# One chunk's transpose moved from TensorE to the DMA crossbar, and the last output tile made in three column pieces

## The chip, the cores and the metric

The kernel runs on one core of a Trainium2 chip. The metric is device time in microseconds (us); lower is better. A core has a matrix engine (TensorE, PE in the profile; its weight loads are the row PEld), a vector engine (DVE), a scalar engine (ACT), GpSimd (POOL) and SyncE (SP). Each works through its own instruction list in order. SP and POOL also start DMA transfers; the transfers then run on the core's 16 DMA engines, beside everything else.

## The reference, cut to what matters

A decaying linear attention feeds a feed-forward block:

```python
# q, k, v: (4 batches, 8 heads, 768 positions, 64) float32
state = gamma[h] * state + k_t (outer) v_t           # per head
y_t   = q_t @ state / sqrt(64)
x     = y as (3072 tokens, 512)
h = x @ w_in                                         # 512 -> 2048
g = h + sin(alpha * h)**2 / (alpha + 1e-9)
out = g @ w_out                                      # 2048 -> 512, float32
```

## The kernel before, in words

The 3072 tokens are 24 chunks of 128, six per batch. Within a chunk the attention is a masked matrix product; between chunks a 64x64 state per head is carried. The list `order` (also called `P`) first names the first chunk of each batch and then the rest, so `P[4]` is the second chunk of batch 0. Chunks are taken in groups of 4, 2, 4, 4, 4, 4 and 2; the last group has the two token tiles that end the kernel.

For a chunk the steps are these:

- **load**: POOL starts one transfer each for q, k and v (L83), which also convert float32 to bf16. q and k of a chunk lie side by side in the tile `qkr`, which has one buffer for each chunk.
- **transpose** of q and k into `qkT` (six buffers in rotation). Two ways exist. `stage_T` (L190 to L200): eight 128x128 transposes on PE into a PSUM tile `pt` (L195), then one copy by DVE (L200) or ACT (L198). `turn` (L202 to L205): one DMA transpose, SBUF to SBUF, started by SP. Before the change the seventh and eighth chunk, `P[6]` and `P[7]`, still go by `stage_T`; from `P[8]` on all go by `turn`.
- **A** (`stage_A`): scores on PE (L213) from `qkT` into `pa`, masked by DVE into `aT` (L217).
- **M** (`stage_M`): the chunk's output on PE (L247, L251), then DVE writes it, scaled, into `xT` (L258), the transposed input of the feed-forward block. **S** adds to the state (L227), and ACT copies it (L234).

The feed-forward work of a group is a `phase`: it runs over slots of one or two 128-row blocks of the hidden layer. A slot has PE products into `ph` (L279), a sine (L282) and a square (L287) on ACT, and a fused multiply-add on DVE into `gT` (L294). Between slots stand the products of the group before with `w_out` (L304, `po`), 16 for each token tile. When a tile's sixteenth is done, `take` has ACT copy it to `o_sb` (L316; three buffers) and SP send it out (L317). The last tile of all is copied in two halves, one by DVE (L313) and one by ACT (L314), into one `o_sb`, and then leaves in one transfer.

The order of all engines' work is written out by hand. Around the change it is: the end of the first group's stage, with the product calls `F(...)` and the transposes of `P[4]` and `P[5]`; then the POOL loads of `P[7]` and on; then `phase(1, ...)`, whose table says which attention step stands in which slot: `T(P[6])` in slot 0, `A(P[6])` in slot 1, `T(P[7])` in slot 2, `A(P[7])` and `M(P[6])` in slot 3, `A(P[8])` and `M(P[7])` in slot 5. The entries `X(P[8])`, `X(P[9])` and so on are `turn` calls, two slots or more ahead of their A.

SP's list before is short: two loads and alpha at the start, the stores of the first three token tiles, then transposes and stores in turn.

Of the kernel before, what the change touches and what calls it, by code (L numbers as in the profile page):

```python
# [8 lines left out]
F32 = mybir.dt.float32  # L9
# [6 lines left out]
def kernel(  # L16
# [15 lines left out]
    nc = tc.nc  # L32
    B, H, S, D = q.shape
    C = 128
# [3 lines left out]
    d_model = H * D  # L38
    d_ff = moe_w_in.shape[1]
    KS = d_model // 128  # L40
    FF = d_ff // 128
# [7 lines left out]
    sizes = [4, 2, 4, 4, 4, 4, 2]  # L49
    assert sum(sizes) == NJ  # L50
    NG = len(sizes)
    groups = [order[sum(sizes[:g]):sum(sizes[:g + 1])] for g in range(NG)]
# [4 lines left out]
    work = ctx.enter_context(tc.tile_pool(name="work", bufs=2))  # L57
    psum = ctx.enter_context(tc.tile_pool(name="psum", bufs=1, space=bass.MemoryType.PSUM))
# [5 lines left out]
    w_out = big.tile([128, FF, d_model], BF16, name="w_out")  # L64
# [125 lines left out]
    def stage_T(j, eng=None, tag="ty"):  # L190
        pt = psum.tile([128, 2 * NP, 128], BF16, name="pt", tag=tag, bufs=4 if tag == "mm" else 1)
        st["qkT", j] = work.tile([128, 2 * NP, 128], BF16, name="qkT", tag="qkT", bufs=6)
        for i in range(2):
            for p in range(NP):
                nc.tensor.transpose(pt[:, i * NP + p, :],  # L195
                                    raw["qk"[i], j][:, 2 * p:2 * p + 2, :].rearrange("p h d -> p (h d)"), ident)
        if eng is nc.scalar:
            nc.scalar.copy(st["qkT", j], pt)  # L198
        else:
            nc.vector.tensor_copy(st["qkT", j], pt)  # L200

    def turn(j):  # L202

        st["qkT", j] = work.tile([128, 2 * NP, 128], BF16, name="qkT", tag="qkT", bufs=6)
        nc.sync.dma_start_transpose(out=st["qkT", j], in_=raw["qk", j].rearrange("p i h d -> p (i h d)"))  # L205

    def stage_A(j):
        qkT = st["qkT", j]
        pa = psum.tile([128, 2, NP, 128], F32, name="pa", tag="pa")
        for p in range(NP):  # L210
            for e in range(2):
                r = slice(64 * e, 64 * e + 64)
                nc.tensor.matmul(pa[:, e, p, :], qkT[r, NP + p, :], qkT[r, p, :],  # L213
                                 start=(p == 0), stop=True, skip_group_check=True)
        aT = work.tile([128, 2, NP, 128], BF16, name="aT", tag="aT", bufs=2)
        m = dec.rearrange("p e n t -> p (e n) t") if j % NCH == 0 else mask_bc
        nc.vector.tensor_mul(aT.rearrange("p e n t -> p (e n) t"), pa.rearrange("p e n t -> p (e n) t"), m)  # L217
        st["aT", j] = aT
# [17 lines left out]
    def stage_M(j):  # L236
        c = j % NCH
        g, i = place[j]
        if g not in xT:
            xT[g] = work.tile([128, KS, sizes[g] * C], BF16, name="xT", tag="xT", bufs=3)  # L240
        qkT, aT, vs = st["qkT", j], st["aT", j], raw["v", j]
        py = psum.tile([128, NP, 128], F32, name="py", tag="ty")
        if c > 0:
            for p in range(NP):
                for e in range(2):
                    r = slice(64 * e, 64 * e + 64)
                    nc.tensor.matmul(py[r, p, :], s_bd[c % 2][:, p, r], qkT[:, p, :],  # L247
                                     start=(p == 0), stop=True, skip_group_check=True)
        for p in range(NP):
            for e in range(2):  # L250
                nc.tensor.matmul(py[64 * e:64 * e + 64, p, :], vs[:, 2 * p + e, :], aT[:, e, p, :],  # L251
                                 start=(c == 0 and p == 0), stop=True, skip_group_check=True)
        x = xT[g][:, :, i * C:(i + 1) * C]
        if c == 0:
            nc.scalar.copy(x, py)
            return
        ps = stage_S(j) if c < NCH - 1 else None
        nc.vector.tensor_mul(x, py, qg[:, c])  # L258
        if ps is not None:
            keep_S(j, ps)  # L260


    gT = {}
# [33 lines left out]
    out_view = out.rearrange("(t p) n -> p t n", p=128)  # L297
# [3 lines left out]
    def ff_out(g, ts, f):  # L301
        if (g, ts) not in po:
            po[g, ts] = psum.tile([128, d_model], F32, name="po", tag="mm", bufs=4)
        nc.tensor.matmul(po[g, ts], gT[g][:, f, ts * C:(ts + 1) * C], w_out[:, f, :],  # L304
                         start=(f == 0), stop=(f == FF - 1))
        if f == FF - 1:
            take(g, ts)

    def take(g, ts):
# [6 lines left out]
            nc.scalar.copy(o_sb, po[g, ts])  # L316
        nc.sync.dma_start(out=out_view[:, groups[g][ts], :], in_=o_sb)  # L317

    def out_pieces(g, tss):
        return [lambda ts=ts, f=f: ff_out(g, ts, f) for ts in tss for f in range(FF)]  # L320

# [53 lines left out]
    def phase(g, outs, att, nf=1):  # L375

        no, done = len(outs), 0
        for n in range(FF // nf):
            now = Slot(g, n * nf, nf=nf).sq("A")
            for fn in att.get(n, ()):  # L380
                fn()
            now.add()
            while done < no * (n + 1) * nf // FF:
                outs[done]()
                done += 1

    def T(j):
        return lambda: stage_T(j)

    def X(j):  # L390
        return lambda: turn(j)

    def A(j):
        return lambda: stage_A(j)

    def M(j):
        return lambda: stage_M(j)

    def SK(j):
        return lambda: keep_S(j, stage_S(j))  # L400
# [3 lines left out]
    P = order  # L404
    n3, n4 = 3 * C, 4 * C
    def F(ts, fs):
        for f in fs:
            for t in ts:
                ff_out(0, t, f)

    def early(f, tag="mm"):
        return Slot(0, f, (0, n3), tag=tag)
# [10 lines left out]
    c = early(3)  # L423
# [10 lines left out]
    c = early(6)  # L434
# [45 lines left out]
    scale_v(P[4], nc.vector)  # L480
    F((0, 1), (13, 14))
    stage_T(P[5], nc.scalar, "mm")
    F((0, 1), (15,))


# [8 lines left out]
    for n in range(11, NJ + 2):  # L494
# [3 lines left out]
        if n in (13, 15):  # L498
            scale_v(P[(n - 9) // 2], nc.gpsimd)

    outs = out_pieces(0, (2, 3))

    def fill(n):
        for _ in range(n):
# [9 lines left out]
    stage_M(P[5])  # L514
    fill(4)
    phase(1, outs,
          {0: [T(P[6]), X(P[8])], 1: [A(P[6])], 2: [T(P[7]), X(P[9])], 3: [A(P[7]), M(P[6])], 4: [X(P[10])],
           5: [A(P[8]), M(P[7])], 6: [X(P[11]), A(P[9]), M(P[8]), SK(e1)], 7: [M(P[9])]}, 2)
    for g in range(2, NG):
        att = {}  # L520
        if g + 1 < NG:
            js = groups[g + 1]
            for i, j in enumerate(js):
                a = i * FF // len(js) + 1
                n = P.index(j) + 2
                if n < NJ:
                    att.setdefault(a + 1, []).append(X(P[n]))
                att.setdefault(a, []).append(A(j))
                if i > 0:
                    att[a].append(M(js[i - 1]))  # L530
                if j % NCH == 1:
                    att[a].append(SK(j - 1))
            att.setdefault(FF - 2, []).append(M(js[-1]))
        phase(g, out_pieces(g - 1, range(sizes[g - 1])), att, 1 if sizes[g] > 2 else 2)
    for fn in out_pieces(NG - 1, range(sizes[-1])):
        fn()
# [1 line left out]
_INS = ['q', 'k', 'v', 'moe_w_in', 'moe_w_out', 'moe_alpha']  # L538
_OUTS = [((3072, 512), 'float32')]
# [25 lines left out]
```

## Time and profile before

| what | value |
|---|---|
| median of 8 runs | 219.77 us (219.16 to 221.38) |
| the profiled execution: its own time | 218.79 us |
| its span, first to last instruction | 217.0 us |
| granted TensorE clock | 0.996 |
| PE busy | 204.5 us (94%) |
| ACT busy | 162.8 us (75%) |
| DVE busy | 128.2 us (59%) |
| POOL busy | 90.0 us (41%) |
| DMA moved | 24.67 MB |

The profile page has a row for each engine over the span cut in 40 slices, a chain of waits followed back from the last instruction, and rows for groups of instructions with their source line (L) and tile names. The time of the profiled execution is 1.79 us more than its span, which is what lies around the first and the last instruction. A timeline row reads: start, duration, engine, line, operation, output<-input, shape, count; and in brackets how long the engine was idle before, and which instruction released it. "SPq" is SP's queue of transfer-starting instructions; the length of such a row is the time that SP spends on starting, not the transfer itself. A transfer's time from issue to landing is given apart.

### The profile page before, as it was taken

The numbers are of one execution on the slowest core, as the hardware profiler recorded it, in microseconds if no ns is written. First come the engines' busy times: TensorE is split into PE (matmuls) and PEld (weight loads), VectorE is DVE, ScalarE is ACT, GpSimd is POOL, SyncE is SP. The second block draws the span as 40 slices with busy tenths as digits, with TensorE's granted clock in tenths as the row PEclk, the third lists the DMA queues.
The fourth block names the chain that finished last, engine by engine and source line by source line (L and its number), as shares of the span: only waits on it lengthen the run. The fifth ranks groups of instructions, "written<-read, shape, count | busy, mean of one in ns | idle before, by whom it ended". The sixth has DMA issues, their size and how long they took to land.

```text
span 217.0 us, 4218 instructions
## 1 busy us (share of the span) xinstructions
PE 204.5 (94%) x1634; PEld 108.0 (50%) x1661; DVE 128.2 (59%) x213; ACT 162.8 (75%) x311; POOL 90.0 (41%) x105
## 2 busy tenths in 40 slices
PE   7999898999989999999999999999999999999992
PEld 3545544467764545445454545454544544556540
DVE  4687669858895767766376466367464655233300
ACT  7679796658989899788768867777868876766610
POOL 8975336899699885994963000000000000000000
PEclk9999999999999999999999999999999999999998
DMA  9999999999999999999999047127011101111121
GB/s 129 152 192 190 205 207 166 154 206 180 154 145 188 162 130 163 110 150 169 133 173 134 17 97 100 47 51 98 15 37 51 48 0 51 48 48 48 51 96 49
DMA packets 99508, 24.67 MB, mean 114 GB/s; under 512 B 92304, under 2 KB 96416, under 8 KB 99488
## 3 DMA queue, kind: packets, MB, share of 16 engines
q0 software_dynamic: 77024, 13.37, 85.3%
q1 hardware_dynamic: 22464, 11.02, 26.7%
q8 instruction: 13, 0.21, 0.5%
q14 instruction: 7, 0.06, 0.1%
HBM read 27.27 MB, written 6.29 MB: 155 GB/s over the span
## 4 chain that ended last, share of the span: by engine, by line
PE 74%; DVE 10%; DMA 4%; POOL 4%; ACT 4%; issue 2%; POOLq 0%
PE po L304 35%; PE ph L279 31%; DVE gT L294 5%; DMA qkr<-in_k_dram 4%; PE py L247 3%; PE pa L213 2%; POOL qkr L83 2%; DVE aT L217 2%; PE py L251 2%; ACT s L282 1%; POOL vr L83 1%; DVE xT L258 1%; ACT s L287 1%; PE ps L227 1%; DVE s L289 1%
## 5 line engine op out<-in xcount | busy, mean ns | idle before, releaser
L294 DVE SCALAR_TENSOR_TENSOR gT<-s,rec_alpha,ph 128x512 bf16<-128x512 f32 (+3 forms) x120 | 74.2, 638 | 68.0 <-ACT s L287 67.4
L279 PE MATMUL ph<-xT,w_in 128*128 128x512 bf16 (+3 forms) x478 | 97.9, 336 | 1.1 <-DVE gT L294 0.7
L304 PE MATMUL po<-w_out,gT 128*128 128x512 bf16 x360 | 94.1, 379 | 3.8 <-issue 2.9
L282 ACT ACTIVATE s<-ph,alpha_sb 128x512 f32<-128x512 f32 (+3 forms) x120 | 69.6, 602 | 33.7 <-PE ph L279 33.5
L279 PEld LDWEIGHTS <-w_in 128*128 128x128 bf16 x480 | 45.6, 98 | 42.6 <-issue 2.4
L287 ACT ACTIVATE s<-s 128x512 f32<-128x512 f32 (+1 forms) x94 | 58.4, 621 | 2.6
L304 PEld LDWEIGHTS <-gT 128*128 128x128 bf16 x384 | 35.2, 98 | 38.2 <-issue 0.6
L112 POOL TENSOR_TENSOR vr<-vr,kg 128x512 bf16<-128x512 bf16 x21 | 22.0, 1058 | 13.4 <-DMA vr<-in_v_dram 13.4
L217 DVE TENSOR_TENSOR aT<-pa,mask 128x1024 bf16<-128x1024 f32 x20 | 24.4, 1222 | 0.3 <-PE pa L213 0.3
L83 POOL DMA_DIRECT2D vr<-in_v_dram x24 | 21.8, 910 | 3.1 <-DMA w_in<-in_moe_w_in_dram 1.7
L83 POOL DMA_DIRECT2D qkr<-in_q_dram x23 | 21.3, 927 | 3.9 <-DMA w_in<-in_moe_w_in_dram 1.7
L83 POOL DMA_DIRECT2D qkr<-in_k_dram x23 | 20.6, 894 | 3.8 <-DMA w_out<-in_moe_w_out_dram 3.4
L234 ACT CAST s_bd<-ps 64x256 bf16<-64x256 f32 x40 | 14.4, 360 | 2.5 <-PE ps L227 2.1
L316 ACT COPY o_sb<-po 128x512 f32<-128x512 f32 x23 | 13.1, 576 | 3.9 <-PE po L304 3.9
L258 DVE TENSOR_TENSOR xT<-py,qg 128x512 bf16<-128x512 f32 x20 | 13.7, 685 | 2.6 <-PE py L251 2.4
L328 PE MATMUL spare<-warm 128*128 128x512 bf16 x27 | 9.9, 490 | 1.4 <-DVE warm L131 1.2
L213 PEld LDWEIGHTS <-qkT 64*128 64x128 bf16 x192 | 5.4, 94 | 9.3 <-issue 7.1
L251 PE MATMUL py<-aT,vr 128*64 128x128 bf16 x192 | 9.5, 220 | 0.4 <-DVE rec_alpha L366 0.2
L213 PE MATMUL pa<-qkT 64*128 64x128 bf16 x192 | 9.5, 219 | 0.2
L247 PE MATMUL py<-qkT,s_bd 128*64 128x128 bf16 x160 | 8.3, 224 | 0.7 <-DVE xT L258 0.7
L247 PEld LDWEIGHTS <-s_bd 128*64 128x64 bf16 x160 | 5.4, 109 | 4.8 <-issue 2.0
L251 PEld LDWEIGHTS <-vr 128*64 128x64 bf16 x192 | 6.9, 110 | 1.3 <-issue 1.0
(59 smaller groups left out, 69.7 us busy)
## 6 DMA issues: line engine op xcount, KB each, us to landing
out_dram<-o_sb SPq DMA_DIRECT2D x24, 256.0 KB, 2.6
vr<-in_v_dram POOLq DMA_DIRECT2D x24, 128.0 KB, 6.7
qkr<-in_q_dram POOLq DMA_DIRECT2D x23, 128.0 KB, 5.8
qkr<-in_k_dram POOLq DMA_DIRECT2D x23, 128.0 KB, 6.2
w_in<-in_moe_w_in_dram POOLq DMA_DIRECT2D x4, 512.0 KB, 10.6
w_out<-in_moe_w_out_dram POOLq DMA_DIRECT2D x4, 512.0 KB, 14.6
q<-in_q_dram SPq DMA_DIRECT2D x1, 256.0 KB, 3.3
k<-in_k_dram SPq DMA_DIRECT2D x1, 256.0 KB, 4.3
```

The costliest lines, as they stand in the source:

```text
L83: nc.gpsimd.dma_start(out=t, in_=chunk_of(src, j))
L112: eng.tensor_mul(raw["v", j], raw["v", j], kg[:, j % NCH, :, None].to_broadcast([128, H, D]))
L213: nc.tensor.matmul(pa[:, e, p, :], qkT[r, NP + p, :], qkT[r, p, :], start=(p == 0), stop=True, skip_group_check=True)
L217: nc.vector.tensor_mul(aT.rearrange("p e n t -> p (e n) t"), pa.rearrange("p e n t -> p (e n) t"), m)
L247: nc.tensor.matmul(py[r, p, :], s_bd[c % 2][:, p, r], qkT[:, p, :], start=(p == 0), stop=True, skip_group_check=True)
L251: nc.tensor.matmul(py[64 * e:64 * e + 64, p, :], vs[:, 2 * p + e, :], aT[:, e, p, :], start=(c == 0 and p == 0), stop=True, skip_group_che ...
L258: nc.vector.tensor_mul(x, py, qg[:, c])
L279: nc.tensor.matmul(self.ph[:, m, :], w_in[:, i, f * 128:(f + 1) * 128], xT[g][:, i, self.lo:self.hi], start=(m == 0 and i == 0), stop=(i = ...
L282: nc.scalar.activation(out=self.s[:, m, :], in_=self.ph[:, m, :], func=ACTF.Sin, scale=alpha_sb[:, f:f + 1])
L287: nc.scalar.activation(out=self.s, in_=self.s, func=ACTF.Square)
L294: nc.vector.scalar_tensor_tensor(gT[self.g][:, f, self.lo:self.hi], self.s[:, m, :], rec_alpha[:, f:f + 1], self.ph[:, m, :], op0=ALU.mult ...
L304: nc.tensor.matmul(po[g, ts], gT[g][:, f, ts * C:(ts + 1) * C], w_out[:, f, :], start=(f == 0), stop=(f == FF - 1))
```

## The change

There are two edits. First, the transpose of `P[6]` leaves slot 0 of phase 1, where PE and DVE did it, and becomes a `turn` that stands in the program just before the last product call of the first stage. In SP's list it comes fourth: after alpha and ahead of all stores. It waits for the landing of q and k of `P[6]` and for its `qkT` buffer, which the first chunk used.

Second, the last token tile is no longer made as one tile of 512 columns but as three of 256, 128 and 128 columns, one after the other, each with its own 16 products over the hidden layer, its own copy (ACT for the first, DVE for the other two) and its own store.

```diff
+    def last_tile(g, ts):
+        lo = 0
+        for n in (d_model // 2, d_model // 4, d_model // 4):
+            c = slice(lo, lo + n)
+            lo += n
+            ph = psum.tile([128, n], F32, name="poh", tag="mm", bufs=4)
+            for f in range(FF):
+                nc.tensor.matmul(ph, gT[g][:, f, ts * C:(ts + 1) * C], w_out[:, f, c],
+                                 start=(f == 0), stop=(f == FF - 1))
+            o_sb = work.tile([128, d_model], F32, name="o_sb", tag="o_sb", bufs=3)[:, :n]
+            if n > d_model // 4:
+                nc.scalar.copy(o_sb, ph)
+            else:
+                nc.vector.tensor_copy(o_sb, ph)
+            nc.sync.dma_start(out=out_view[:, groups[g][ts], c], in_=o_sb)
...
     F((0, 1), (13, 14))
     stage_T(P[5], nc.scalar, "mm")
+    turn(P[6])
     F((0, 1), (15,))
...
-          {0: [T(P[6]), X(P[8])], 1: [A(P[6])], 2: [T(P[7]), X(P[9])], 3: [A(P[7]), M(P[6])], 4: [X(P[10])],
+          {0: [X(P[8])], 1: [A(P[6])], 2: [T(P[7]), X(P[9])], 3: [A(P[7]), M(P[6])], 4: [X(P[10])],
...
-    for fn in out_pieces(NG - 1, range(sizes[-1])):
+    for fn in out_pieces(NG - 1, range(sizes[-1] - 1)):
         fn()
+    last_tile(NG - 1, sizes[-1] - 1)
```

The `turn` that the first edit calls exists before:

```python
def turn(j):
    st["qkT", j] = work.tile([128, 2 * NP, 128], BF16, name="qkT", tag="qkT", bufs=6)
    nc.sync.dma_start_transpose(out=st["qkT", j], in_=raw["qk", j].rearrange("p i h d -> p (i h d)"))
```

## The prediction

> **What bounds the kernel now.** I read the engine rows first, then the chain of waits, then the two places that the change touches.
>
> ```profile
> PE 204.5 (94%) x1634; PEld 108.0 (50%) x1661; DVE 128.2 (59%) x213; ACT 162.8 (75%) x311; POOL 90.0 (41%) x105
> ...
> PE 74%; DVE 10%; DMA 4%; POOL 4%; ACT 4%; issue 2%; POOLq 0%
> ```
>
> PE is busy for 94% of the span and is 74% of the chain that ended last. Time is won by taking work off PE where the chain runs on it, or by shortening the tail behind its last product. The first place, in the chain in order of time:
>
> ```profile
> 46.87 0.97 PE po L304 x4
> 47.84 0.87 PE ph L279 x8
> 48.71 0.45 PE pt L195 x8
> 49.16 0.43 PE po L304 x2
> 49.59 0.87 PE ph L279 x8
> 50.47 0.33 PE pa L213 x8
> ```
>
> The row `pt` is the transpose of P[6]. It lies on the chain between PE pieces that follow without a gap, so its 0.45 us count in full. The row `pa` is A of P[6], the first reader of the transpose. The second place, in the timeline:
>
> ```profile
> 212.28 0.59 PE L304 MATMUL po<-w_out,gT 128*128 128x512 bf16 x2
> 212.91 0.42 DVE L313 COPY o_sb<-po 128x256 f32<-128x256 f32 x1 [6.23 <-PE po L304]
> 213.37 0.37 ACT L314 COPY o_sb<-po 128x256 f32<-128x256 f32 x1 [3.33 <-DVE o_sb L313]
> 213.77 0.33 SPq L317 DMA_DIRECT2D out_dram<-o_sb  x1
> ```
>
> PE ends at 212.87. The two half copies run one after the other, not side by side: ACT starts 0.04 us after DVE ends. So 0.90 us pass between the last product and the store's issue. The span ends 3.2 us later.
>
> **Part 1: the transpose.** Removed on PE: eight products, 0.45 us on the chain. Removed on DVE: one copy of 128x1024 (0.69 us at 49.20); in this stretch DVE waits for ACT (0.40 us at 50.28), so that alone is worth nothing. ACT waits 0.24 to 0.29 us for PE in each of these slots, and so follows PE forward. A of P[6] would be due on PE at 50.39 - 0.45 = 49.94, if its input is there.
>
> Added: one DMA transpose on SP. It waits for q and k of P[6]; POOL issued k at 35.31 and it took 7.0 us to land, so 42.31 (q: 32.76 + 8.7 = 41.46). The buffer it waits for is old. The nearest case, P[9], had k at 45.33 + 5.9 = 51.23 and its transpose started at 51.31, 0.08 later; so here the start is 42.39. Behind it on SP stand the first two stores (issued at 42.99 before). SP spends 1.24 to 2.6 us on starting a transpose, so they slip by 0.6 to 2.0 us. Nobody feels it: PSUM is freed by ACT's copy, and a fourth use of the three `o_sb` buffers comes only at 64.99. The third store (48.49) and the transpose of P[8] behind it (49.00) keep their place.
>
> When does it land? The query of the transpose nearest in time (49.0, of P[8]) says:
>
> ```profile
> L205 SPq DMA_TRANSPOSE qkT<-qkr x1: 1613/1613/1613, 49.0 to 49.0; - x1
> ...
> DMA to landing us min/median/max: 7.9/7.9/7.9
> ```
>
> The others between 51 and 81 us took 5.7 to 7.5; those after 115, with the DMA engines nearly idle, 3.1 to 5.2. At 42.39 the engines are as full as at 49 (loads moved at a steady 154 GB/s from 36 to 46 us; a load takes 6.2 to 7.4 us to land). **Here a rule speaks otherwise**: the Trainium skill (Advanced Engine Details and Errata, X-Bar Transpose) says that transposing DMAs on this chip are as fast as ordinary ones. An ordinary one of the same 256 KB, the store at 42.99, took 5.5; by the rule the transpose lands at 47.9 and A never waits (gain 0.45). The rows say that a transpose is slower: 3.1 to 5.2 against the 2.0 of a store in quiet, 7.9 against 4.1 of the store issued 0.5 us before it at 48.49. I take the row: 42.39 + 7.9 = 50.3. The lower end is 5.7 (48.1). The upper end is the slowest quiet one plus what the crowd added to the store: 5.2 + (5.9 - 2.0) = 9.1 (51.5).
>
> So A of P[6] waits 50.3 - 49.94 = 0.36 us on PE, in order, with the `po` and `ph` of slots 1 and 2 queued behind it; of the 0.45 won, 0.09 stay. Ends: 0.45 won, or 51.5 - 50.39 = 1.1 lost.
>
> The second cost is on the next transposes. The new one moves 256 KB more; of one in quiet I see about 1.3 us of moving at 205 GB/s. The engines are shared until 57, where P[8]'s transpose lands (49.00 + 7.9 = 56.9) while its A starts on PE at 57.62, and at 57.5 with 0.09 us won. If the whole 1.3 us reach it, it lands at 58.2 and PE waits 0.7; if half, at 57.55, and it waits 0.05. DVE needs these scores only at 58.75, 0.72 us after PE had them, since it is busy itself, and that takes up much. I take 0.1, ends 0 and 0.7. P[9] (51.31 + 7.3 = 58.6, due at 60.06) has 1.4 us, P[10] (56.95 + 6.3 = 63.2) is due at 66.8. The loads of P[7] (k at 38.12 + 6.9 = 45.0, used at 52) bear it.
>
> Part 1 in sum: 0.45 - 0.36 - 0.1 = nothing; ends 0.45 won and 1.8 lost. What is won or lost here shifts all that follows, since no transfer bounds the chain after it.
>
> **Part 2: the tail.** On PE 16 products of 512 columns at 216 ns (18 `po` in 4.06 us) are 3.46 us. In their place come 16 of 256 at 108 ns (`ph` of slots with two blocks: eight in 0.87) and 32 of 128. For these the first stage has a row with the same weights and width:
>
> ```profile
> 24.88 1.06 PE L279 MATMUL ph<-xT,w_in 128*128 128x128 bf16 x16
> ```
>
> (1.06 - 0.22)/15 = 56 ns, 0.22 being one product alone. **A rule speaks against the change here**: the Trainium skill (TensorE: Matmul & The Clock Gate, Back-to-back issue gap) gives 81 ns for a sustained stream of weight load and 128-column product, and 56 only for one without the weight load. This row has a weight load for each product and still shows 56, in a run of 16; the new run is 32 long. By the row: 1.73 + 1.79 = 3.52, 0.06 more than before. By the rule: 1.73 + 2.59 = 4.32, 0.86 more, which would eat the gain. I take the row.
>
> The last product then ends at 212.93. DVE's copy of 128x128 isn't in the trace; from 0.42 (128x256) and 0.69 (128x512, `xT`) it is some 0.29. With 0.03 and 0.04 us between engines the last store is issued at 213.29, not 213.77: 0.48 won. The first two pieces' copies and stores lie under later products (their stores at about 211.6 and 212.4, 0.33 each on SP). The third piece's `o_sb` is the one that tile 0's store read, issued at 210.1 and landed 2.0 later, at 212.1, before the copy at 212.96.
>
> The last transfer shrinks from 256 KB, which the trace shows moving for 0.70 us, to 64 KB, in 128 rows of 512 B where it had 2 KB. At the same rate that is 0.18; no row shows 512 B rows here, and if they cost half again to twice as much, 0.27 to 0.36. I take 0.30, so 0.40 won; the ends are 0 (time goes by rows, not bytes) and 0.52. What follows the data (0.4 us to landing, about 1.2 us of ending) stays. Part 2: 0.48 + 0.40 = 0.9 won; ends 0.45 and 1.0 by the rows, 0.1 by the rule.
>
> **Sum.** 218.79 - 0.0 - 0.9 = 217.9 for an execution like the profiled one. That one lies 0.98 under the median of 219.77, so the median goes to about 218.9; I say 219.0, a gain of 0.8 us (0.35%). A measurement of this kernel can tell about 0.5%, 1.1 us, from no change.
>
> **The rivals.**
> 1. *The transpose is in time* (landing by 49.9, 7.5 us after issue). For it: most rows of the busy time are 5.7 to 7.5. Against: none of those stood in front of so many loads. 0.45 + 0.9 = 1.35 won: 218.4.
> 2. *The transpose becomes the wait* (slower than before). Place: the first weight load of A of P[6] on PE, behind which slots 1 and 2 stand. Price: each us of landing past 49.94 is one us of PE. It decides when it takes away the tail's 0.9 too, past 51.3 (8.9 us after issue); slower by 1.1 from 52.4. For it: loads ahead of it in the engines, and the stores issued beside it moved no data until about 46. Against: nothing in the trace took over 7.9. At the upper ends (1.8 lost, 0.9 won) the median is 220.7.
> 3. *The tail gives nothing*: 32 short products at 81 ns. Then 0.1 won with part 1 at nothing: 219.7. Against it is the row of 16.
> 4. *The last store is no shorter* than before: part 2 is 0.5, median 219.3, still no change that can be told.
>
> **Numbers.** Forecast 0.40, rival 1 0.23, rival 2 0.22, rival 3 0.07, rival 4 0.08. Faster by over 0.5%: most of rival 1 and a little of the forecast's edge, 0.26. Slower: the far part of rival 2, 0.19. The rest 0.55. The range goes from rival 1 with the best tail (219.77 - 0.45 - 1.0 = 218.3, less 0.3 for the spread of medians, 218.0) to rival 2 at its upper ends, 220.8.
>
> **What would show it.** In the profile after: no `pt` at 48.7 on PE; SP's transpose at about 42.4 with a landing near 7.9; a wait of PE on L213 near 50 us of 0.3 to 0.4 (0 in rival 1, over 1.5 in rival 2); A of P[8] waiting 0 to 0.2; the last 32 products in about 1.8 us (2.6 in rival 3); the last store issued 0.36 us after PE's end, and the span ending about 2.8 us after that. The forecast is wrong if A of P[6] waits over 1 us, or if the time from PE's end to the span's end does not shrink from 4.1 to about 3.2.

## The result, and the profile after

The changed kernel takes 218.35 us (median of 20 runs, 217.5 to 219.33) where the kernel before takes 219.58 (55 runs). The ratio is 0.9941, with a 95% interval of 0.9926 to 0.9957: 0.6% faster, 1.2 to 1.3 us. 219.0 was forecast, a gain of 0.8. The 0.5% that was named as the least that can be told from no change lies inside the interval's gains of 0.43 to 0.74% (the medians alone give 0.9944).

Where it came from can be read to a tenth of a microsecond, once the profiled execution is cut at three events that both kernels have. They are the first `ph` product of phase 1, the first `ph` product of the next group, and ACT's copy of the last tile but one. "Start" is all before the first event; the tail ends with the span, which is printed to a tenth, so tails are good to 0.05 us.

| profiled execution | start | stage (phase 1) | middle | tail | span |
|---|---|---|---|---|---|
| before | 47.68 | 16.87 | 144.91 | 7.54 | 217.0 |
| changed | 48.62 | 16.72 | 144.90 | 6.46 | 216.7 |

The spans alone mislead. The changed kernel's profiled execution had a start that was 0.94 us longer and still ended 0.3 us sooner. The start varies from execution to execution with or without the edits: three other kernels below that have the first edit started at 47.68 to 47.70, and two that do not have it there, e1 and e5, at 48.26 and 48.80. Without it the gains are 0.15 in the stage and 1.08 in the tail, 1.23 in sum, as in the medians (219.58 - 218.35 = 1.23; that they agree to the hundredth is chance).

**The stage.** PE's weight loads from `qkT` in the changed kernel's timeline, for A of P[6], P[7], P[8] and P[9]. The bracket is the idle time of the weight loads and what ended it:

```profile
50.89 0.23 PEld L213 LDWEIGHTS <-qkT 64*128 64x128 bf16 x8 [0.21 <-issue]
...
54.67 0.22 PEld L213 LDWEIGHTS <-qkT 64*128 64x128 bf16 x8 [0.50 <-DVE qkT L200]
...
58.57 0.22 PEld L213 LDWEIGHTS <-qkT 64*128 64x128 bf16 x8 [0.37 <-DMA qkT<-qkr]
...
61.29 0.23 PEld L213 LDWEIGHTS <-qkT 64*128 64x128 bf16 x8 [0.50 <-DMA qkT<-qkr]
```

and before the change, for P[6] and P[7]:

```profile
50.39 0.23 PEld L213 LDWEIGHTS <-qkT 64*128 64x128 bf16 x8 [0.21 <-issue]
...
53.89 0.23 PEld L213 LDWEIGHTS <-qkT 64*128 64x128 bf16 x8 [0.21 <-DVE qkT L200]
```

An idle time of 0.21 us stands before A even where nothing was waited for ("issue"): A then starts 0.97 us after the first of the `ph` products just ahead of it, without a gap on PE. So only what lies above 0.21 is delay.

A of P[6] did not wait for its transpose. It ran 2.27 us after the stage began, where it was 2.71 before (50.39 - 47.68): the whole 0.44 were won there. The transpose itself was quick:

```profile
L205 SPq DMA_TRANSPOSE qkT<-qkr x1: 1347/1347/1347, 43.8 to 43.8; - x1
...
DMA to landing us min/median/max: 6.6/6.6/6.6
```

43.84 + 6.6 = 50.4, some 0.45 us before A of P[6] started. But A of P[7] then stood at 0.50, for the DVE copy of the other PE transpose. That is a delay of 0.29 us, and 0.15 us of the gain were left (54.67 - 48.62 = 6.05 against 53.89 - 47.68 = 6.21). DVE's own timeline says why the copy could not come sooner. In the changed kernel:

```profile
51.23 0.87 DVE L294 SCALAR_TENSOR_TENSOR gT<-s,rec_alpha,ph 128x256 bf16<-128x256 f32 x2 [2.81 <-ACT s L287]
52.02 1.22 DVE L217 TENSOR_TENSOR aT<-pa,mask 128x1024 bf16<-128x1024 f32 x1
53.15 0.86 DVE L294 SCALAR_TENSOR_TENSOR gT<-s,rec_alpha,ph 128x256 bf16<-128x256 f32 x2
53.93 0.69 DVE L200 COPY qkT<-pt 128x1024 bf16<-128x1024 bf16 x1
```

and before, the first and the last of these four:

```profile
50.28 0.87 DVE L294 SCALAR_TENSOR_TENSOR gT<-s,rec_alpha,ph 128x256 bf16<-128x256 f32 x2 [0.40 <-ACT s L287]
...
52.99 0.68 DVE L200 COPY qkT<-pt 128x1024 bf16<-128x1024 bf16 x1
```

DVE first sat for 2.81 us, because its next instruction waits for the first slot's sine and square. These depend on a `ph` product that stands ahead of the removed transpose, so nothing made them earlier. From there DVE worked without a gap through these rows to the copy. Counted from the stage's begin, the first of them starts at 2.61 us (2.60 before) and the copy ends at 6.00 (5.99 before). PE had come forward; DVE had not. Before, A of P[7] started at 6.21, so this copy had about 0.2 us to spare; the 0.44 us that PE won were more than that, and the rest became the delay.

**The tail.** The changed kernel's timeline:

```profile
210.04 3.70 PE L327 MATMUL poh<-w_out,gT 128*128 128x256 bf16 x48
...
212.38 2.10 SPq L334 DMA_DIRECT2D out_dram<-o_sb  x3
...
213.83 0.29 DVE L333 COPY o_sb<-poh 128x128 f32<-128x128 f32 x1 [0.60 <-PE poh L327]
```

PE's 48 products take 3.70 us with the 0.22 of one alone: no sign of a slow stream of short ones. The last copy takes 0.29 (0.90 before for the two half copies in turn). The last of SP's three stores starts at 212.38 + 2.10 - 0.33 = 214.15, 3.91 us after ACT's copy of the tile before (210.24), against 4.31 before (213.77 - 209.46): 0.40 won. From issue to landing, before and in the changed kernel:

```profile
DMA to landing us min/median/max: 2.0/2.0/2.0
...
DMA to landing us min/median/max: 1.6/1.6/1.6
```

By the trace's time stamps these are 2.03 and 1.55 us: 0.48 more. The rest, 0.21 by the same stamps, lies behind the landing (1.23 us to the end of the span before, 1.02 now), where no gain was expected. At the end SP waits once for each of eight semaphores, which its transfers use in rotation. The waits from the landing on, before and in the changed kernel:

```profile
L560 SPq EVENT_SEMAPHORE  x6: 28/28/28, 215.8 to 216.1; - x6
...
L579 SPq EVENT_SEMAPHORE  x3: 28/28/28, 215.7 to 215.8; - x3
```

Three more transfers put the last one three places further on in the rotation, so that three waits, about 0.06 us each, fall away. The kernels below start different numbers of transfers and bear this out: from the last landing to the end of the span it is 1.17 us with five such waits (e2), 1.08 with four (e1, e6), 1.02 to 1.04 with three (the changed kernel, e3, e5, e8, e9, e12) and 0.96 to 0.98 with two (e4, e7, e10, e11). So a part of the gain, 0.2 us, comes from the number of transfers alone. That is luck, not design.

### The profile page after: what moved, and what is told of

It reads as the page before. It is cut to its first block, busy times and chain, and to the rows that moved or that the text cites. A ratio compares the mean times of both kernels' runs of the same rounds, so it can differ in the third digit from the quotient of the medians.

```text
span 216.7 us, 4276 instructions
## 1 busy us (share of the span) xinstructions
PE 204.1 (94%) x1658; PEld 109.2 (50%) x1685; DVE 128.2 (59%) x213; ACT 162.4 (75%) x311; POOL 90.1 (42%) x105
## 4 chain that ended last, share of the span: by engine, by line
PE 70%; DMA 12%; DVE 7%; POOL 5%; issue 3%; ACT 2%; POOLq 0%; DVEq 0%
PE po L304 31%; PE ph L279 29%; DMA qkr<-in_k_dram 8%; DMA vr<-in_v_dram 4%; PE pa L213 3%; PE py L247 2%; DVE aT L217 2%; POOL qkr L83 2%; PE poh L327 2%; DVE gT L294 2%; PE py L251 2%; DVE xT L258 1%; POOL vr L83 1%; ACT s L282 1%; ACT s L287 1%
## 5 line engine op out<-in xcount | busy, mean ns | idle before, releaser
L304 PE MATMUL po<-w_out,gT 128*128 128x512 bf16 x344 | 90.7, 380 | 3.8 <-issue 2.9
L304 PEld LDWEIGHTS <-gT 128*128 128x128 bf16 x368 | 33.6, 98 | 36.4 <-issue 0.6
```

## The experiments

For all of them, the same cuts of the profiled execution:

| kernel | start | stage | tail | ratio to before (95%) |
|---|---|---|---|---|
| changed | 48.62 | 16.72 | 6.46 | 0.9941 (0.9926 to 0.9957) |
| e1 tail only | 48.26 | 16.88 | 6.56 | 0.9965 (0.9947 to 0.9983) |
| e2 transpose only | 50.44 | 16.71 | 7.44 | 1.0009 (0.9991 to 1.0028) |
| e3 P[7] a slot earlier | 47.70 | 16.94 | 6.46 | 0.9942 (0.9926 to 0.9958) |
| e4 P[7] by the crossbar too | 48.07 | 18.98 | 6.43 | 1.0048 (1.0021 to 1.0075) |
| e5 transpose started late | 48.80 | 25.29 | 6.50 | 1.0345 (1.0298 to 1.0391), two runs |
| e6 tail 256, 256 | 47.69 | 16.72 | 6.79 | 0.9959 (0.9937 to 0.9981) |
| e7 tail 256, 128, 64, 64 | 48.32 | 16.72 | 6.76 | 0.9944 (0.9923 to 0.9964) |
| e8 e3 and P[8] sooner | 47.68 | 16.43 | 6.48 | 0.9926 (0.9898 to 0.9955), six runs |
| e9 P[8] sooner alone | 48.29 | 16.71 | 6.50 | one run, 218.17 us |
| e10 e7 with own buffers | 48.29 | 16.71 | 6.40 | 0.9945 (0.9925 to 0.9965) |
| e11 e8 and e10 | 48.05 | 16.43 | 6.42 | 0.9932 (0.9909 to 0.9954) |
| e12 e8 again | 48.53 | 17.84 | 6.52 | 0.9928 (0.9906 to 0.9950), six runs |

The middle is 144.90 to 144.92 us in every one. So what an edit does to its stretch reaches the end unchanged. The times tell less: the intervals of e1, e3, e6, e7, e8, e10, e11 and e12 all overlap the changed kernel's. What is said below of differences between these rests on the stretches.

### The two edits apart

e1, against the changed kernel:

```diff
-    turn(P[6])
...
-          {0: [X(P[8])], 1: [A(P[6])],
+          {0: [T(P[6]), X(P[8])], 1: [A(P[6])],
```

> The kernel before with the second edit alone (last tile in three pieces); P[6] is transposed on PE as before. Theory (the tail is most of the gain): from the start of ACT's copy of the next to last tile (L316) to the end of the span 7.54 us before, 6.46 in the changed kernel, and 6.4 to 6.5 here; the time 1.0 to 1.1 us under the kernel before, ratio about 0.995. Rival (the transpose brings its full 0.45 us and the tail only 0.85): ratio 0.996, and the same stretch at 6.7. A second rival, that the tail's gain hangs on the first edit through the store queue, would leave the stretch at over 7.

e2, against the kernel before:

```diff
+    turn(P[6])
     F((0, 1), (15,))
...
-          {0: [T(P[6]), X(P[8])], 1: [A(P[6])],
+          {0: [X(P[8])], 1: [A(P[6])],
```

> The kernel before with the first edit alone (P[6] by the DMA crossbar). Theory (the 0.45 us freed on PE are mostly given back two slots later, where A of P[7] waits for DVE's copy of the PE transpose of P[7]): from the first ph product of phase 1 to the first ph product of group 2 it is 16.87 us before and 16.72 in the changed kernel; here 16.6 to 16.8, with a PE wait of 0.4 to 0.5 us on L213 for DVE L200, ratio 0.999. Rival 1 (full gain): the stretch at 16.4, ratio 0.998. Rival 2 (the transpose is late in most runs): a wait on L213 for the transpose at A of P[6], the stretch over 17, ratio over 1.001.

The stretches came out as the theory said. The tail alone gives 6.56, 0.98 of the 1.08; the rest is mostly the one semaphore wait more. The transpose alone gives a stage of 16.71, with A of P[7] held up by DVE's copy as in the changed kernel. By the ratios the tail alone wins 0.35% and the transpose alone can't be told from nothing. So the tail is most of the gain; the transpose's 0.16 us show in the profiles (16.87 and 16.88 without it, 16.71 or 16.72 in e2, e6, e7, e9, e10 and the changed kernel) and not in the times.

The two ratios multiply to 0.9974, not to the 0.9941 of both edits together. The stretches do add up, so what is missing lies in the starts or in the spread of the runs. An estimate of the start, from the median time less 1.8 us (what time and span differ by) and less the other three stretches, is 48.5 us before and in the changed kernel, 48.4 in e1 and 48.8 in e2. The changed kernel has e2's edit and not its longer start, so e2's 0.3 us looks like a draw of its 14 runs; that is not shown. The start of e2's execution, 50.44, is another matter and is taken up at the end.

### Was the DVE copy the wait that took the gain?

e3, against the changed kernel as all that follow, calls P[7]'s PE transpose a slot earlier:

```diff
-          {0: [X(P[8])], 1: [A(P[6])], 2: [T(P[7]), X(P[9])],
+          {0: [X(P[8])], 1: [A(P[6]), T(P[7])], 2: [X(P[9])],
```

> The changed kernel with the PE transpose of P[7] called one slot earlier (after A of P[6] in slot 1), so that its DVE copy stands ahead of the fused multiply-add of slot 1. Theory (that copy was the wait that took the gain): PE's 0.5 us wait on L213 for DVE L200 goes, the stretch from the first ph of phase 1 to the first ph of group 2 falls from 16.72 to 16.3 to 16.5, and the time falls by 0.2 to 0.4 us against the changed kernel, ratio to the kernel before about 0.9925. Rival (DVE is the bound there in any order): another wait of the same size takes its place, the stretch stays at 16.7, ratio 0.994.

Half right. The wait for the copy went: A of P[7] ran 5.76 us after the stage began instead of 6.05. But the stage did not get shorter. The weight load of A of P[8] in e3's timeline:

```profile
58.28 0.17 PEld L213 LDWEIGHTS <-qkT 64*128 64x128 bf16 x6 [1.29 <-DMA qkT<-qkr]
```

P[8]'s transpose, started at 49.00 as before, took 9.2 us to land instead of 7.9. A of P[8] ran 10.58 us into the stage, where it was 9.94 before. The next wait behind the copy came from the added transpose itself, whose 256 KB move ahead of P[8]'s: in the profiles in which P[8]'s transpose follows P[6]'s at the old place (the changed kernel, e2, e3, e6, e7, e10) it took 8.6 to 9.2 us to land, and 7.7 and 7.9 in the two without P[6]'s (e1 and before).

e8 therefore starts P[8]'s transpose ahead of the third store, when its k has landed:

```diff
     load_chunk(P[8])
+    turn(P[8])
...
-          {0: [X(P[8])], 1: [A(P[6])], 2: [T(P[7]), X(P[9])],
+          {1: [A(P[6]), T(P[7])], 2: [X(P[9])],
```

> The changed kernel with the PE transpose of P[7] one slot earlier, and the DMA transpose of P[8] started by SP ahead of the third store instead of behind it (about 47.6 us instead of 49.0, as soon as k of P[8] has landed). Theory (with the DVE copy out of the way, the gain was handed to the landing of P[8]'s transpose, for which A of P[8] waited 1.3 us): the wait on L213 for the transpose falls under 0.3, the stretch from the first ph of phase 1 to the first ph of group 2 falls from 16.94 to 16.3 to 16.5, and the time is 0.2 to 0.4 us under the changed kernel (ratio to the kernel before about 0.992). Rival (DVE is the bound of this stage from P[8] on, whatever comes in time): the stretch stays at 16.7 or more, ratio 0.994.

The stage is 16.43: all of the 0.44 us. e9 has this edit without P[7]'s:

> The changed kernel with only the start of P[8]'s transpose moved ahead of the third store. Theory: A of P[8] no longer waits for its transpose (0.37 to 0.47 us before), but the 0.5 us for DVE's copy of P[7] stay, and DVE is what A of P[8] feeds; the stretch stays at 16.6 to 16.75. Rival (that landing already sets the stage in the changed kernel): the stretch falls under 16.5.

Its stage is 16.71. A of P[8] no longer waited for its transpose (it ran 0.16 us sooner, at 9.79), the 0.50 for the copy stood, and the length was the changed kernel's. So in the changed kernel the copy sets the stage, and the late landing of P[8] costs nothing until the copy is out of the way. e11 takes e8's stage and the tail of e10 below:

> All three together: P[7] one slot earlier, P[8]'s transpose ahead of the third store, and the four-piece tail with its own buffers. If the gains add: stretch of the stage 16.3 to 16.5, tail 6.2 to 6.3, time 0.4 to 0.7 us under the changed kernel, ratio to the kernel before about 0.991. If the stage is bound by DVE: 0.2 under, ratio 0.993.

Stage and tail add up, 16.43 and 6.42; the ratio, 0.9932, misses the 0.991 that was expected and is no better than e8's. e8 once more:

> The same kernel as in e8, for a narrower interval. If the stage's 0.44 us are real, the stretch of the stage is again 16.3 to 16.5 and the ratio to the kernel before lies at 0.9925, 0.3 us under the changed kernel's 0.994; if e8 was a lucky draw of starts, the stretch is the same but the ratio is 0.994 or more.

The ratio, 0.9928, was near the expected one, but the stage of this execution missed, at 17.84. A of P[9] waited 2.27 us: k of P[9] landed 9.7 us after its issue, and its transpose, which needs it, started at 55.97, where e8's started at 54.24 (before the change: 5.9 us, and 51.31). e8's order leaves P[9] no margin; it stood at 0.61 even in e8's first execution. Both ratios of this kernel lie under the changed kernel's 0.9941, and all three intervals overlap. That it is the better kernel is not shown by the times.

### What a late landing costs

e5 starts the same transpose behind the third store:

```diff
-    turn(P[6])
...
-          {0: [X(P[8])], 1: [A(P[6])],
+          {0: [X(P[6]), X(P[8])], 1: [A(P[6])],
```

> The changed kernel with the transpose of P[6] started late, by SP behind the third store (about 49 us) instead of ahead of the first; nothing else changes. Theory (rival 2 of the prediction: each us of landing past A's due time is one us of PE): it lands 7 to 9 us after issue, at about 57; A of P[6] was due 2 slots after, so PE waits 6 to 7 us on L213 and the time is 5 to 7 us over the changed kernel. Rival (the stage has slack that takes it up): under 3 us over.

PE's wait for a transpose in e5 (us in total, times, the longest):

```profile
PEld L213 <- DMA qkT<-qkr: 7.5, 1, 7.5
```

7.5 us of waiting (7.3 of it delay), and a stage of 25.29, 8.6 longer than the changed kernel's; the time is 227.05. The mechanism of the prediction's second rival is real, and dearer than one for one (the last section says why). What kept it away is that the transpose started at 43 and not at 50. e4 gives the next chunk to the crossbar as well:

```diff
     load_chunk(P[8])
+    turn(P[7])
...
-          {0: [X(P[8])], 1: [A(P[6])], 2: [T(P[7]), X(P[9])],
+          {0: [X(P[8])], 1: [A(P[6])], 2: [X(P[9])],
```

> The changed kernel with P[7] by the crossbar too; its transpose is started by SP behind the first two stores, about 46 to 47 us. Theory (a landing of 6.6 to 8.6 us): it lands at 53 to 55, A of P[7] is due on PE at about 53.7 and waits 0 to 1.3 us for it; 0.45 us of PE and 0.7 of DVE are freed; the transposes of P[8] and P[9] land later in their turn, and A of P[8] waits 1 us more. Net between 0.5 faster and 1.0 us slower than the changed kernel; ratio to the kernel before 0.992 to 0.999. Rival (landing does not matter since PE has slack here): 0.6 to 0.9 faster than the changed kernel, ratio 0.991.

It is worse than expected: slower than the kernel before. P[7]'s transpose started at 46.06 and landed 9.2 us later, at 55.3, where P[6]'s had taken 6.9; A of P[7] stood at 2.18 us, 1.97 of it delay. The second of two transposes in a row landed later; how much of that is the first one's doing and how much that of the loads at that time was not tried.

### The tail's terms

e6 makes two pieces of 256:

```diff
-        for n in (d_model // 2, d_model // 4, d_model // 4):
+        for n in (d_model // 2, d_model // 2):
...
-            if n > d_model // 4:
+            if lo < d_model:
```

> The changed kernel with the last tile in two pieces of 256 columns instead of 256, 128, 128 (ACT copies the first, DVE the second). Theory (the gain is the copy behind the last product plus the size of the last store): DVE's copy is 0.42 us instead of 0.29, the last store moves 128 KB instead of 64, PE is 0.06 shorter; from ACT's copy of the next to last tile to the end of the span 6.5 to 6.7 us instead of 6.46, and 0.1 to 0.2 us slower than the changed kernel. Rival (the size of the last store is what counts, by the byte): 0.35 us slower and more.

e7 cuts the last 128 columns once more:

```diff
-        for n in (d_model // 2, d_model // 4, d_model // 4):
+        for n in (d_model // 2, d_model // 4, d_model // 8, d_model // 8):
```

> The changed kernel with the last 128 columns cut once more into 64 and 64 (four pieces). Theory (short products are bound by the weight load, about 55 ns each): PE needs 32 x 55 = 1.76 us for the last 128 columns instead of 0.90, so the stretch from ACT's copy of the next to last tile to the end is 7.1 to 7.3 us, 0.6 to 0.8 over the changed kernel. Rival (products go by their columns, 64 in 28 ns): PE needs the same 0.9, the copy and the store are shorter, and the stretch is 6.3 to 6.4.

e6 is 0.33 us over the changed kernel in the tail (0.30 by the time stamps), more than the theory's 0.1 to 0.2 and under the rival's 0.35: 0.13 by the longer copy, 0.16 by the landing (1.71 against 1.55), 0.06 by one semaphore wait more, less 0.04 on PE. In e7 PE took 3.74 us for all 64 products, so the 32 of 64 columns went by their width, about 28 ns each by estimate from this, with no sign of their weight loads: the theory was wrong and the rival right on PE. Still the tail was 6.76, for another reason:

```profile
214.00 0.23 DVE L333 COPY o_sb<-poh 128x64 f32<-128x64 f32 x1 [0.68 <-DMA out_dram<-o_sb]
```

The fourth piece's `o_sb` was the first piece's, and that store had not yet landed. e10 gives the two short pieces buffers of the idle tile `s`:

```diff
-            o_sb = work.tile([128, d_model], F32, name="o_sb", tag="o_sb", bufs=3)[:, :n]
+            if n < d_model // 4:
+                o_sb = work.tile([128, 1, 512], F32, name="s", tag="s", bufs=5)[:, 0, :n]
+            else:
+                o_sb = work.tile([128, d_model], F32, name="o_sb", tag="o_sb", bufs=3)[:, :n]
```

> The changed kernel with the last 128 columns cut into 64 and 64, the two last pieces copied into buffers that no store is reading. Theory (the fourth copy of the four-piece tail was late by 0.5 us because its buffer was still being read by the first piece's store): that wait goes, the stretch from ACT's copy of the next to last tile to the end falls from 6.76 to 6.2 to 6.3 us, 0.2 under the changed kernel's 6.46. Rival (SP's 0.33 us for each store, four in a row, takes the place of the wait): 6.4 to 6.5.

The wait is gone, but the tail is 6.40, the rival's value. The last copy and the last two stores in its timeline:

```profile
213.34 0.86 SPq L337 DMA_DIRECT2D out_dram<-s  x2
213.48 0.22 DVE L336 COPY s<-poh 128x64 f32<-128x64 f32 x1 [0.24 <-PE poh L327]
```

The last store started 0.11 us after its copy had ended (213.70 to 213.81), where the changed kernel's followed in 0.03, because SP was still on the one before: two starts in a row on SP came 0.42 and 0.47 us apart here, as the first two stores of the kernel do (42.99 and 43.5). So it started 3.91 us after ACT's copy, no sooner than the changed kernel's; what the tail won is a landing 0.06 us shorter and one semaphore wait less. With pieces this short, the starting of stores is the limit.

## Why the prediction was right or wrong

The forecast of a small gain, within its range, held; the measured 1.2 to 1.3 us lie nearer to rival 1 (1.35) than to the forecast (0.8), and 0.6% is on the side of the 0.5% to which only 0.26 had been given. By its steps:

- **0.45 us off PE: right.** A of P[6] came 0.44 us sooner.
- **"ACT ... follows PE forward": wrong, and this is the step that failed.** It was taken from ACT's short waits for PE in each slot. In the first slot ACT waits for a product that is not behind the transpose, so neither ACT nor DVE, which waits for ACT, came forward there. The sum has no term for the DVE copy of P[7], which in the profile before had only some 0.2 us to spare. It took 0.29 of the 0.44. Rival 1 shared this mistake: the transpose was in time, and still 0.15 and not 0.45 stayed. e3 and e8 show the step: with the copy earlier, and P[8]'s transpose too, the whole 0.44 come out.
- **Landing after 7.9 us: too slow.** It was 6.5 to 6.9 in the eleven profiles of kernels that start it between 42.6 and 44.2 us; the wait of 0.36 did not happen. The row nearest in time was not the nearest case: P[8]'s transpose has a store just ahead of it on SP and P[6]'s has none. That this makes the difference is argued, not tried: in e8 and e9 P[8]'s transpose has no store just ahead of it and still took 7.7 and 8.0, but there it follows P[6]'s. The Trainium skill's rule of equal speed (Advanced Engine Details and Errata, X-Bar Transpose; 5.5 us, from the store) was off by about as much on the other side (1.1 against 1.3), and the conclusion drawn from it, no wait, was the right one.
- **The next transposes: right in size, short in reach.** P[8] landed 0.7 us later, as the half of 1.3 that was taken. It delayed A of P[8] by 0.16 (0.37 less the 0.21 of every A), near the 0.1 that was taken, but at no cost, as e9 shows; DVE's slack of 0.72 can take it up. "The loads ... bear it" was too short: k of P[9] took about 7.6 us in place of 5.9, P[9]'s transpose started 2.3 us later against the stage's begin, and its A was held up by 0.29 (0.50 less 0.21).
- **Part 1 in sum**: nothing forecast, 0.15 measured in the profile. It is near for the wrong reasons, and so by luck: a wait that did not come and one that cost nothing stood in the sum for one that was not in it.
- **Short products at 56 ns: right**, and the 81 ns that the Trainium skill gives for such a stream (TensorE: Matmul & The Clock Gate, Back-to-back issue gap) wrong here: 48 products took 3.70 us, where 81 ns for the 32 short ones would by estimate have made it 4.5 (4.32 and the 0.22 of one alone).
- **The last copy and store**: 0.48 forecast to the store's start, 0.40 measured; 0.40 for the smaller store, 0.48 measured. From PE's end to the span's end it is 3.0 us, where 3.2 was forecast and 4.1 stood before.
- **"What follows the data ... stays": wrong by 0.21.** It is the count of semaphore waits, three fewer at 0.06 us.
- **Rival 2** did not come to pass, but e5 and e4 show it at work as soon as the start is later or a second transpose follows. Rivals 3 and 4 fell.

## What to carry to other kernels

When work is taken off the bounding engine, look at what each other engine was waiting for at that point: those that hang on something ahead of the removed work don't come forward, and the first of their results that the bounding engine needs takes the gain back, but for what slack it had. A DMA that replaces engine work has a due time, and so has every transfer queued behind it; one early transpose was free here, a second cost 2 us (a part of it by the clock, below). A tail shortens by cutting the last piece small in width, until its buffers or the start of its stores become the wait.

## What the runs showed of the hardware that was not expected

**A late transfer costs more than its wait, sometimes.** Stretches of e4 from A of P[7]'s wait on: the length, the busy time of PE, PEld, DVE, ACT and POOL, then the granted clock, DMA share and GB/s:

```profile
54.00:55.00 1.00, 0.00 (x0) 0.00 (x0) 0.59 (x2) 0.97 (x3) 0.00 (x0) 1.00 1.43 228
...
56.00:57.00 1.00, 1.00 (x23) 0.66 (x18) 1.00 (x2) 0.49 (x2) 0.00 (x0) 0.87 1.60 159
57.00:58.00 1.00, 1.00 (x7) 0.67 (x6) 1.00 (x4) 0.24 (x1) 0.00 (x0) 0.50 1.69 157
...
59.00:60.00 1.00, 1.00 (x5) 0.57 (x4) 0.00 (x0) 0.97 (x3) 0.32 (x1) 0.50 2.51 150
60.00:61.00 1.00, 1.00 (x15) 0.67 (x13) 0.64 (x2) 0.46 (x2) 1.00 (x2) 0.92 2.27 168
```

PE idles for 1.9 us, is back at 55.4, and more than a microsecond later, while it is busy, runs at half clock for some 3.4 us. In e5 the clock fell 3.8 us into the gap and was at half from about 55 to 62 us, the last 3.4 us of it after the wait. There lies what makes a wait of 7.5 cost 8.6: from A of P[6] to A of P[7] it took 5.09 us, and 3.78 in the changed kernel. The Trainium skill (TensorE: Matmul & The Clock Gate, Why this matters for your kernels) warns of idle gaps over about 3 us, as in e5; in e4 1.9 were followed by the same. But e12's gap of 2.0 us left the clock at 1.00, so the length of the gap alone does not decide; what else does stays open.

**The start is where executions differ.** It ran from 47.68 to 50.44 us in these profiles, while the middle stayed the same to 0.02. In e2, PE had idled 1.65 us before 19.6 us, for the load of a chunk's q, and the clock was at half from 21.3 to 24.7. That is most of why its profiled span, 219.5, looks so slow, and why spans were compared by stretches here.

**A smaller store lands only a little sooner**: 256 KB in 2.0 us, 128 KB in 1.7, 64 KB in 1.6, 32 KB in 1.5. The rows became shorter with the pieces, so bytes and row length are not told apart.
